# Rescheduled side steps in a fused attention and token-mixing kernel: an added stop and an early drain in the last groups, a later third weighing part in the first, two more warm-up matmuls

## The chip, the cores and the metric

The kernel runs on one core of a Trainium2 chip. The metric is the device time of one execution in microseconds (us), the median of several runs. Engines are called TensorE (PE; its weight loads are PEld), VectorE (DVE), ScalarE (ACT), GpSimd (POOL) and SyncE (SP, which here only issues DMAs).

## What is computed

x is 2048 tokens by 1024, in bf16. It is normalised row by row, and three things are added:

```
xn  = layernorm(x)
out = x + A(xn) + B(xn)

B: h = layernorm(xn)                        # [2048, 1024]
   u = gelu(h.T @ w1 + b1)                  # [1024, 3584]
   y = u @ w2 + b2                          # [1024, 2048], transposed back

A: q, k, v = xn @ wq, xn @ wk, xn @ wv      # 32 heads of 32, 4 segments of 512 tokens
   per segment s:  p = softmax(q k.T * scale + causal mask)
                   a_dot = p v
                   a_mem = phi(q) M / (phi(q) z + 1e-6)
                   o_s = g * a_mem + (1 - g) * a_dot,  g = sigmoid(beta)
                   M += phi(k).T v;  z += sum(phi(k))
   phi(t) = t + 1 for t > 0, exp(t) else
   A = concat(o_s) @ wo
```

## The kernel before, in words

**Stages.** One core does all of it in one program. First come warm-up matmuls on a tile of zeros (N_WARM of them, 512 columns each, lines 529 to 531), while x and the first columns of w1 arrive. The layer norm makes h chunk by chunk, and the first hidden columns are multiplied as chunks come (early_hidden: 16 chunks, 8 matmuls for each in eight PSUM banks). Then the token-mixing products follow (two large matrix products in a seven-product scheme) up to about 351 us. The rest is attention, the function that the change edits.

**Attention.** A unit u is one segment (u // 8) and one group of four heads (u % 8), 32 units in all. TensorE's work for a unit is of two kinds:

- The unit's own attention: logits(u, step) writes four banks (0 to 3) with q k.T, ScalarE takes the exponential of them into pT (line 1216), and GpSimd clears what the causal mask forbids (line 1220). weigh(u, part), for part 0, 1 and 2, multiplies pT with the values, and from segment 1 on also pqT (phi of q) with the memory MZbf. Parts 0 and 2 use bank 4, part 1 uses bank 5. Each part ends with a VectorE copy from the bank to ost (line 1267); part 2 also updates the memory M in the first three segments. weigh(u - 1, ...) runs in unit u, one unit late.
- Dense jobs of eight 512-column matmuls each, kept in a queue (jobs): q_job and k_job (projections for unit u + 2), v_job, and wo_job(c, half), half of the output projection of token chunk c. Jobs take banks 6 and 7 in turn. Each job ends with a copy out of its bank: ScalarE for q and most v, VectorE for k (kT, line 1112), for the v of m = 1 and 2 (vA, line 1142), and for the output job (fin, line 1158, a sum with the rest of the result; its second half then issues the output DMA and loads the fin of two chunks later).

**Side steps.** The small VectorE work that follows weigh is a queue of closures, side. For unit u - 1 in segments 1 to 3 combine gives four: scales (three small operations, lines 1308 to 1310), products(0) and products(1) (prod, line 1314), and add (o_s, line 1320), which also issues the DMA that transposes o_s into oT. In segment 0 there are two. Between the first and the rest stands phi_q(u) (lines 1080 and 1082, the result is pqT, which weigh(u, 0) reads one unit later). At the end come phi_k(u + 1) with the DMA transpose into pk, and in some units the scaling of a chunk of x for the next segment (xs, line 986) with its DMA transpose (xn). From u = 23 on the phi_k step is still queued but does nothing.

**What sets the order.** The order is written out by the program as it is built; each engine then runs its own list in that order. dense(n) issues n matmuls of the queue of jobs. Where side is not empty and dense was not called with side=False, it stops within a job at the places that the job's stops name, after 1, 4 and 7 matmuls (STOPS) or after 1 and 4 (STOPS_DVE), and takes one step from side at each. A unit's matmuls are cut into pieces by the shares given to cut, and logits and weigh stand between the pieces: cuts[0], logits 0, cuts[1], weigh 0, cuts[2], weigh 1, cuts[3], weigh 2, then the new steps are queued, cuts[4], logits 1, and so on. Only cuts[0] and what follows weigh 2 may take steps. Steps that find no stop are left over for the next unit.

**Output jobs.** Those of segment 2 (chunks 8 to 11) run in units 27 to 31: chunk 8 in 27 and 28, 9 in 29 and 30, 10 in 30 and 31, 11 in 31. After unit 31 what is left in side is issued, and tail() does the last unit's weighing, combine and transposition, and the output products of segment 3. Its first two products, into banks 6 and 7, need the oT of groups 24 to 29; the next ones that of 30, and the last that of 31.

A wait is set per tile and per bank: an operation waits for the last writer of what it reads and for the readers of what it overwrites.

Of the kernel before, what the change touches and what calls it, by code (L numbers as in the profile page):

```python
# [30 lines left out]
N_UNIT = N_SEG * N_GRP  # L31
# [353 lines left out]
class _Kernel:  # L385
    SB_BASE = 16512
    SB_END = 229344
    LEAD = 2
    N_WARM = 10
    G_AT = 3584  # L390
    B_AT = G_AT + 7 * 14336

# [104 lines left out]
    def consts(self):  # L497
# [31 lines left out]
        with fw.group(reads=[self.R_warm], writes=[self.R_bank[0]]):  # L529
            for _ in range(self.N_WARM):  # L530
                fw.mm(self.bank(0), self.warm[:, 0:P], self.warm[:], start=True, stop=True)
# [617 lines left out]
    def wo_job(self, c, half):  # L1149
        s = c // 4  # L1150

        def mm(b, j):
            self.fw.mm(self.bank(b), self.oT[s % 2][:, j, (c % 4) * P:(c % 4 + 1) * P],
                       self.wo[:, j, half * 512:(half + 1) * 512], start=(j == 0), stop=(j == N_GRP - 1))

        def end(b):
            dst, R = self.fin[c % 4][:, half * 512:(half + 1) * 512], self.R_fin[c % 4][half]
            self.fw.op("dve", lambda e: e.tensor_tensor(dst, self.bank(b), dst.bitcast(F16), op=ALU.add),  # L1158
                       reads=[self.R_bank[b], R], writes=[R])
            if half == 1:  # L1160
                self.fw.dma(self.out_d[:, c, :], self.fin[c % 4][:], reads=self.R_fin[c % 4], is_output=True)
                self.load_fin(c + 2)

        return [0, None, lambda: [self.R_wo] + self.R_oT[s % 2], mm, end, self.STOPS_DVE]

    def load_fin(self, c):
        if c < N_TCH:
# [186 lines left out]
    def attention(self):  # L1354
        self.jobs, self.turn = deque(), 0
        self.side = deque()
        self.exps, self.in_etmp = [], [None] * 4
        self.wo_plan = {}
        for s in range(N_SEG - 1):
            at = [N_GRP * s + 10 + n for n in range(8)] if s < 2 else [27, 28, 29, 30, 30, 31, 31, 31]  # L1360
            for n, u in enumerate(at):
                self.wo_plan.setdefault(u, []).append((4 * s + n // 2, n % 2))
        self.jobs.extend([self.q_job(0), self.k_job(0)] + [self.v_job(0, c) for c in range(4)])
        self.dense(16)
        self.late_exps()
        self.phi_k(0)
        self.k_transpose(0)
        self.jobs.extend([self.q_job(1), self.k_job(1)])
        self.dense(100)
        self.load_fin(0)  # L1370
        self.load_fin(1)
        for u in range(N_UNIT):
            even = u % 2 == 0
            self.jobs.extend(self.unit_jobs(u))
            total = 8 * len(self.jobs) - sum(j[0] for j in self.jobs)
            c = 4 * (u // N_GRP + 1) + u % N_GRP
            xn = u % N_GRP < 4 and c < N_TCH
            if xn:
                self.xn_load(c)
            cuts = self.cut(total, (0, 4, 2, 2, 2, 14, 8) if even else (7, 3, 2, 2, 2, 16))  # L1380
            self.dense(cuts[0])
            self.logits(u, 0)
            self.dense(cuts[1], False)
            if u:
                self.weigh(u - 1, 0)
            self.dense(cuts[2], False)
            if u:
                self.weigh(u - 1, 1)
            self.dense(cuts[3], False)
            if u:  # L1390
                self.weigh(u - 1, 2)
                steps = self.combine(u - 1)
                last = steps[-1]
                steps[-1] = lambda u=u, last=last: (last(), self.o_transpose_dma(u - 1))
                self.side.append(steps.pop(0))
            if N_GRP <= u:
                self.side.append(lambda u=u: self.phi_q(u))
            if u:
                self.side.extend(steps)
            if u + 1 < N_UNIT:  # L1400
                self.side.append(lambda u=u: (self.phi_k(u + 1), self.k_transpose(u + 1)))
            if xn:
                self.side.append(lambda c=c: (self.xn_scale(c), self.xn_transpose(c)))
            self.dense(cuts[4])
            self.logits(u, 1)
            if even:
                self.dense(cuts[5])
                self.logits(u, 2)
            self.dense(100)
        while self.side:  # L1410
            self.side.popleft()()
        self.tail()
# [82 lines left out]
```

## Time and profile before

| what | value |
|---|---|
| runs | 663.57, 663.70, 662.08 us; median 663.57 |
| the profiled execution's own time | 663.34 us |
| its span (first to last instruction) | 661.6 us |
| mean granted TensorE clock | 0.997 |
| TensorE busy | 646.4 us (98%) |
| VectorE busy | 426.3 us (64%) |
| ScalarE, GpSimd busy | 276.0 us (42%), 144.9 us (22%) |
| attention starts, ends | about 351 us, 661.6 us |

The span is that of one profiled execution; the time of an execution is a little longer (1.74 us here). A row of a group or of the order of time names line, engine, operation and the tiles written and read; ps_all is PSUM. All matmuls carry line 198, that of a helper, so they are told apart by their tiles: "ps_all<-wo,oT" is an output job, "ps_all<-vA,pT" a weighing, "ps_all<-qT,kT" logits, "ps_all<-warm" the warm-up. Matmuls overlap: one of 512 columns is shown with 379 ns, but the next starts 0.216 us after it. Some matmul records are missing from the trace, so that a count can be one or two short. "[0.39 <-DVE kT L1112]" after a row means that the engine was idle for 0.39 us before it, until that instruction released it.

### The profile page before, as it was taken

The numbers are of one execution on the slowest core, as the hardware profiler recorded it, in microseconds if no ns is written. First come the engines' busy times: TensorE is split into PE (matmuls) and PEld (weight loads), VectorE is DVE, ScalarE is ACT, GpSimd is POOL, SyncE is SP. The second block draws the span as 40 slices with busy tenths as digits, with TensorE's granted clock in tenths as the row PEclk, the third lists the DMA queues.
The fourth block names the chain that finished last, engine by engine and source line by source line (L and its number), as shares of the span: only waits on it lengthen the run. The fifth ranks groups of instructions, "written<-read, shape, count | busy, mean of one in ns | idle before, by whom it ended". The sixth has DMA issues, their size and how long they took to land.

```text
span 661.6 us, 11057 instructions
## 1 busy us (share of the span) xinstructions
PE 646.4 (98%) x4567; PEld 303.1 (46%) x4622; DVE 426.3 (64%) x821; ACT 276.0 (42%) x297; POOL 144.9 (22%) x181
## 2 busy tenths in 40 slices
PE   8999999999999999999999999999999999999978
PEld 3444444444444444444444444444444444544434
DVE  6965675665643554244522576689888998777875
ACT  7442232332300000000012777886676776667730
POOL 2500000000020222112220333333333333233320
PEclk9999999999999999999999999999999999999989
DMA  9704242242647645755285687558545685444133
GB/s 318 192 0 128 64 118 73 65 127 64 165 137 206 159 122 133 192 167 135 66 223 183 164 176 115 127 132 174 128 113 118 160 157 127 120 104 85 47 119 96
DMA packets 187242, 87.65 MB, mean 132 GB/s; under 512 B 116024, under 2 KB 174392, under 8 KB 187192
## 3 DMA queue, kind: packets, MB, share of 16 engines
q1 hardware_dynamic: 187048, 86.91, 52.2%
q8 instruction: 36, 0.59, 0.4%
q14 instruction: 14, 0.11, 0.0%
q10 hardware_dynamic: 144, 0.03, 0.0%
HBM read 67.13 MB, written 8.39 MB: 114 GB/s over the span
## 4 chain that ended last, share of the span: by engine, by line
PE 94%; DVE 2%; DMA 2%; issue 1%; ACT 1%; SPq 0%; DVEq 0%
PE ps_all L198 94%; DMA xs<-in_A_x_dram 1%; DMA w1early<-in_B_w_dram 1%; ACT pT L1216 1%; DVE fin L1442 1%; DMA oT<-o_s 0%; DVE vA L1142 0%; DVE ost L1267 0%; SPq L220 0%; DVE fin L1158 0%; DVE xs L986 0%; DVE o_s L1320 0%; DVE pqT L1082 0%; DVE mtmp L1080 0%; DVE prod L1314 0%
## 5 line engine op out<-in xcount | busy, mean ns | idle before, releaser
L1216 ACT ACTIVATE pT<-ps_all 128x2048 bf16<-128x2048 f32 x80 | 150.1, 1876 | 57.4 <-PE ps_all L198 57.3
L1220 POOL TENSOR_SCALAR_AFFINE_SELECT pT<-pT 128x512 bf16<-128x512 bf16 x128 | 96.4, 770 | 197.4 <-ACT pT L1216 197.4
L690 DVE TENSOR_TENSOR part<-ps_all,part 128x512 f32<-128x512 f32 x76 | 52.5, 691 | 119.0 <-PE ps_all L198 118.2
L926 POOL TENSOR_TENSOR part<-part,stg 128x512 f32<-128x512 f32 x24 | 33.0, 1402 | 266.2 <-DVE part L690 266.2
L695 ACT ACTIVATE part<-ps_all 128x512 f32<-128x512 f32 x20 | 11.9, 597 | 149.0 <-PE ps_all L198 149.0
L742 ACT ACTIVATE g<-part,b1c 128x512 f16<-128x512 f32 x36 | 26.0, 722 | 98.9 <-DVE part L690 98.9
L198 PE MATMUL ps_all<-wo,oT 128*128 128x512 bf16 (+2 forms) x254 | 62.8, 374 | 4.1 <-DMA oT<-o_s 3.1
L198 PE MATMUL ps_all<-wv,xnT 128*128 128x512 bf16 x238 | 65.2, 379 | 1.6 <-issue 0.6
L198 PE MATMUL ps_all<-xnT,wq 128*128 128x512 bf16 x248 | 62.0, 380 | 0.8 <-DVE kT L1112 0.4
L1267 DVE CAST ost<-ps_all 128x396 bf16<-128x396 f32 (+2 forms) x96 | 44.6, 476 | 26.8 <-PE ps_all L198 25.1
L198 PE MATMUL ps_all<-xnT,wk 128*128 128x512 bf16 x245 | 59.6, 379 | 1.5 <-issue 1.4
L198 PEld LDWEIGHTS ps_all<-vA,pT 128*128 128x128 bf16 x1280 | 45.0, 96 | 21.4 <-DVE ost L1267 4.4
L198 PE MATMUL ps_all<-g,sum 128*128 128x512 f16 x224 | 51.0, 379 | 0.0
L198 PE MATMUL ps_all<-g,w2s 128*128 128x512 f16 x224 | 51.0, 379 | 0.0
L198 PE MATMUL ps_all<-vA,pT 128*128 128x33 bf16 x1280 | 48.6, 178 | 1.4 <-DVE pqT L1082 1.0
L198 PE MATMUL ps_all<-gT,sum 128*128 128x512 f16 x224 | 49.7, 379 | 0.0
L198 PE MATMUL ps_all<-h,sum 128*128 128x512 f16 x192 | 45.2, 379 | 0.0
L198 PE MATMUL ps_all<-h,w1s 128*128 128x512 f16 x192 | 44.9, 379 | 0.0
L198 PE MATMUL ps_all<-hT,sum 128*128 128x512 f16 x192 | 43.6, 379 | 0.0
L1314 DVE TENSOR_TENSOR prod<-ost,srec 128x512 bf16<-128x512 bf16 x48 | 39.6, 826 | 0.8
L198 PEld LDWEIGHTS ps_all<-xnT,wk 128*128 128x128 bf16 x256 | 23.8, 98 | 29.8 <-issue 3.2
L198 PEld LDWEIGHTS ps_all<-wo,oT 128*128 128x128 bf16 x272 | 23.8, 99 | 29.1 <-issue 11.2
(99 smaller groups left out, 806.0 us busy)
## 6 DMA issues: line engine op xcount, KB each, us to landing
w2s<-in_B_w_dram SPq DMA_DIRECT2D x8, 1792.0 KB, 8.5
w1s<-in_B_w_dram SPq DMA_DIRECT2D x12, 1024.0 KB, 5.6
wq<-in_A_wq_dram SPq DMA_DIRECT2D x32, 256.0 KB, 3.3
wk<-in_A_wk_dram SPq DMA_DIRECT2D x32, 256.0 KB, 3.3
stg<-in_A_x_dram SPq DMA_DIRECT2D x16, 256.0 KB, 2.9
xs<-in_A_x_dram SPq DMA_DIRECT2D x16, 256.0 KB, 3.4
out_dram<-stg SPq DMA_DIRECT2D x16, 256.0 KB, 3.0
fin<-out_dram SPq DMA_DIRECT2D x16, 256.0 KB, 3.6
```

The costliest lines, as they stand in the source:

```text
L198: ins = self.nc.tensor.matmul(*args, **kwargs)
L690: self.fw.op("dve", lambda e: e.tensor_tensor(self.tmp[dst][:], self.bank(b), self.tmp[src][:], op=ALU.add), reads=[self.R_bank[b], self.R ...
L695: self.fw.op("act", lambda e: e.activation(self.tmp[dst][:], self.bank(b), ACT.Copy), reads=[self.R_bank[b]], writes=[self.R_tmp[dst]])
L742: self.fw.op("act", lambda e: e.activation(self.gB[f % 2][half][:, f // 2, :], src, ACT.Gelu_apprx_tanh, bias=self.b1c[:, f:f + 1], scale= ...
L926: fw.op("pool", lambda e: e.tensor_tensor(self.tmp[t][:], self.tmp[t][:], self.stg[k][:, 512 * half:512 * half + 512], op=ALU.add), reads= ...
L1216: fw.op("act", lambda e: e.activation(dst, src, ACT.Exp, scale=SCALE), reads=self.R_bank[0:4], writes=[R[v % 2][kb] for v, kb, _ in blocks ...
L1220: fw.op("pool", lambda e: e.affine_select(d, d, pattern=[[0, 4], [1, P]], compare_op=ALU.is_ge, fill=0.0, base=0, channel_multiplier=-1), ...
L1267: fw.op("dve", lambda e: e.tensor_copy(dst, src), reads=[self.R_bank[b]], writes=[self.R_ost[o][part]])
L1314: fw.op("dve", lambda e: e.tensor_tensor(self.prod[:, n, :], ost[:, n, 0:D_HEAD], rec[:, n].unsqueeze(2).to_broadcast([P, 16, D_HEAD]), op ...
L1442: fw.op("dve", lambda e: e.tensor_tensor(dst, self.ps[:, b, c0:c1], dst.bitcast(F16), op=ALU.add), reads=[self.R_bank[b], R], writes=[R])
```

## The change

There are four edits. N_WARM goes from 10 to 12. The output jobs of chunks 9 to 11 take STOPS, with a stop after the seventh matmul, in place of STOPS_DVE. In units 0 to 9 the shares of cut put two more matmuls between the second and the third weighing part: cuts become 0, 3, 1, 4, 0, 10, 6 (before: 0, 3, 1, 2, 2, 10, 6) in even units and 5, 3, 1, 3, 1, 11 (before: 5, 3, 1, 1, 2, 12) in odd ones, of 24 matmuls. In units 28 to 31 the piece between logits 0 and the first weighing part may take steps, and what then still stands in side is issued ahead of the first weighing part.

```diff
-    N_WARM = 10
+    N_WARM = 12
...
-        return [0, None, lambda: [self.R_wo] + self.R_oT[s % 2], mm, end, self.STOPS_DVE]
+        return [0, None, lambda: [self.R_wo] + self.R_oT[s % 2], mm, end, self.STOPS if c >= 9 else self.STOPS_DVE]
...
-            cuts = self.cut(total, (0, 4, 2, 2, 2, 14, 8) if even else (7, 3, 2, 2, 2, 16))
+            if u < 10:
+                cuts = self.cut(total, (0, 4, 2, 4, 1, 13, 8) if even else (7, 3, 2, 4, 1, 15))
+            else:
+                cuts = self.cut(total, (0, 4, 2, 2, 2, 14, 8) if even else (7, 3, 2, 2, 2, 16))
+            end = u >= N_UNIT - 4
             self.dense(cuts[0])
             self.logits(u, 0)
-            self.dense(cuts[1], False)
+            self.dense(cuts[1], end)
+            while end and self.side:
+                self.side.popleft()()
             if u:
                 self.weigh(u - 1, 0)
```

## The prediction

> **What bounds the kernel now.** I read the share lines of the page first, then the chain of waits from 615 us to the end, the table by stage with the granted clock, and TensorE's order of time in the first groups and in the first 10 us.
>
> ```profile
> PE   8999999999999999999999999999999999999978
> PE 94%; DVE 2%; DMA 2%; issue 1%; ACT 1%; SPq 0%; DVEq 0%
> ```
>
> TensorE is the bound: only its waits, and its time at half clock, can be won. Those at the end:
>
> ```profile
> 630.25 0.69 DVE fin L1158
> ...
> 632.64 0.70 DVE pqT L1082
> 633.35 0.05 issue
> 633.39 1.84 PE ps_all L198 x46
> ...
> 638.33 0.73 DVE o_s L1320
> 639.06 0.03 DVE fin L1158
> 639.09 2.43 DMA oT<-o_s
> 641.52 0.25 issue
> 641.76 5.18 PE ps_all L198 x39
> ```
>
> First column start, second length. Before 633.39 weigh(30, 0) waits for pqT of group 30, whose two VectorE operations stand behind an output job's fin. Before 641.76 the tail's first product waits for oT of group 29, whose add (o_s) ended at 639.06.
>
> ```profile
> 632.20:633.40 1.20, 0.18 (x2) 0.01 (x1) 1.17 (x3) 1.20 (x1) 0.26 (x1) 1.00 0.00 0
> 638.50:641.76 3.26, 0.19 (x1) 0.03 (x1) 3.16 (x8) 0.00 (x0) 1.05 (x2) 0.99 0.30 79
> 641.76:645.13 3.37, 3.37 (x8) 1.14 (x9) 1.28 (x3) 0.00 (x0) 0.00 (x0) 0.50 0.52 157
> ```
>
> Stretch, length, busy PE, PEld, DVE, ACT, POOL, then the granted clock. After the idle 3.26 us the clock is 0.50 for 3.37 us. The same half rate stands at the start, where no clock record exists, in the spacing of the weight loads, 0.43 us until 10.13 and 0.21 after:
>
> ```profile
> 9.71 0.15 PEld L198 LDWEIGHTS ps_all<-h,w1early 128*128 128x128 bf16 x1 [0.28 <-DVE ln_st L588]
> 10.13 0.81 PEld L198 LDWEIGHTS ps_all<-h,w1early 128*128 128x128 bf16 x4 [0.28 <-issue]
> ```
>
> And in the first groups (third weighing part is the x16; the x1 before it is the projection's matmul):
>
> ```profile
> 374.00 0.38 PE L198 MATMUL ps_all<-xnT,wq 128*128 128x512 bf16 x1
> 374.47 0.57 PE L198 MATMUL ps_all<-vA,pT 128*128 128x33 bf16 x16
> ...
> 387.59 0.97 DVE L986 TENSOR_SCALAR xs<-xs,ln_mv,ln_rs 128x1024 bf16<-128x1024 bf16 x1 [1.95 <-DMA xs<-in_A_x_dram]
> 388.48 0.68 DVE L1112 CAST kT<-ps_all 128x512 bf16<-128x512 f32 x1
> ...
> 389.30 0.38 PE L198 MATMUL ps_all<-xnT,wq 128*128 128x512 bf16 x1 [0.39 <-DVE kT L1112]
> ```
>
> A 512-column matmul takes 0.216 us of TensorE (start to start), so 374.00 could have been followed at 374.22: 0.25 us of waiting for the ost copy that frees bank 4.
>
> [...] 10.25, 641.72 and 645.13 are whole multiples of 3.413 us apart (185 and 1). [...] the add at 638.33 stands behind prod at 637.61 and fin at 637.00. [...] o_s takes 0.73 us while POOL's select runs (638.33) and 0.41 without (628.26).
>
> **The change part by part.** I wrote out the order of both versions by hand from dense, cut and STOPS.
>
> *Last groups.* Groups 28 and 29 keep their order, as the job of chunk 9 in group 29 has only an empty step to hand out. From group 30: add28 runs in the stretch before weigh(29, 0); scales29, phi_q30, prod0 and prod1 of 29 all fall in group 30, add29 in the first matmul of group 31, and the five steps of 30 in group 31. Before, group 31 began with six steps left over, and group 30's own came only ahead of the tail.
> - pqT of 30: VectorE has scales29 (0.74 us) and phi_q30 (0.97) done by about 629.5, before weigh(30, 0) is reached at 632.2. The 1.18 us at 633.39 goes.
> - oT of 29: add29 at about 631.3 behind prod1 and fin of wo10.0; with issue to landing 2.4 us, landed near 634.2. The 3.24 us ahead of 641.76 goes, and with it the half clock: 12 products took 4.24 us (641.76 to 646.00) in place of 12 x 0.216 = 2.59, so 1.65.
> - New: add28 (0.42) now precedes the ost copy of weigh(29, 0), which ended just in time for weigh(29, 2) at 625.69: 0.07. fin of wo10.1 (0.61 to its successor) now stands at 632.5 ahead of the ost copy of weigh(30, 0): weigh(30, 2) waits 0.22, as at 619.69 (0.22, same pair).
> - New: the tail's second product writes bank 7, which the last output job leaves (120 jobs alternate 6 and 7). Its fin stands behind prod0, prod1 and add of 30. From ost30 2 at 634.45: scales 0.8, phi 0.95, fin of wo11.0 0.65, two prods 1.4 to 1.8, add 0.4 to 0.7, fin 0.7 ends at 639.5 to 640.2. The first product is through at 638.95, so a wait of 0.55 to 1.3; I take 0.9.
> Sum: 1.18 + 3.24 + 1.65 - 0.07 - 0.22 - 0.9 = 4.9 us, between 4.4 and 5.3. Hidden: phi_q31 and oT of 30 (landed about 642, wanted after 645). SP's queue gets oT of 29 and of 30 ahead of the output DMAs of chunks 10 and 11 that they followed; those reads are wanted after 648. What is late next is that fin.
>
> *First groups (units 0 to 9).* The part two matmuls (0.43 us) later covers the 0.25 us waits in units 1, 5 and 7 and the 0.12 in unit 3: 0.87. The steps each start a stop or two later; in units 1 and 3 the xn step is left to the next unit. So xs for chunk 6 is loaded ahead of xn5's transpose on SP (1.3 us, issued 380.45) in place of behind it, and its landing at 387.6 comes some 1.5 us earlier. That takes all or nothing of the 0.54 us wait at 389.30; I take 0.4. The pk transposes come about 0.65 us later; that of group 2 was issued at 379.13, lands within 5 us, and is used at 390.57. Units 10 to 12 carry one step more, in by unit 13: nothing, as VectorE idles 28 us between 436 and 624 (159.33 of 187.70 busy); without that, one prod, 0.83. In even units the vA cast (0.69) now comes ahead of the third ost copy; no TensorE wait is behind it until the next unit. Sum 1.3, between 0.5 and 1.4.
>
> *Warm-up.* Ten end at 5.70, TensorE idles 1.06 us and starts at 6.76 when w1early lands (6.67). Two more at 0.43 end at 6.55, so they lie in idle time and cost nothing (were it gone, 0.85). What they can bring: the window 3.43 to 6.84 was idle 31% and did not release the clock; it would be idle 6%. If that passes, the release comes at 6.84 and not at 10.25: 3.41 / 2 = 1.7 us. The data would keep up (chunk 1 of h is ready at 8.44, needed at 6.76 + 8 x 0.216 = 8.49; w1early for chunk 2 lands at 9.41, needed at 10.2). [...] Bounds 0 and 1.8; I take 1.6 as the likelier.
>
> **Sum.** The profiled execution is 663.34 us, 661.6 of span and 1.74 around it. It holds both half-rate stretches, and lies 0.2 below the median of the runs, 663.57; the run at 662.08 may have missed one. 663.34 - 4.9 - 1.3 - 1.6 = 655.5; I add 0.4 for small waits of the size of those found at 619.69 that I did not see: 655.9.
>
> **The rivals.**
> - *No earlier release.* All the rest holds, the clock still comes at about 10.2 us: 655.9 + 1.6 = 657.5. For it: whether 6% idle passes is not in the trace. Chance 0.32.
> - *The wait moves to bank 7.* VectorE's chain of group 30 slips by 2 to 3 us [...], TensorE idles near 3.4 us between the first two products, and half clock comes with it: 655.9 + 2.5 + 1.6 = 660. Against it: VectorE has idle time at 629 to 630 in the trace. Chance 0.10.
> - *The change does not do what it says.* The third stop finds no step, "none left over" fails (add29 is left over still), and only the first groups gain: 662. Chance 0.03.
> - *Slower.* The later phi_k steps send the pk transposes so late that weigh part 2 waits in each of the ten first units. Decides once pk comes over 6 us later than now; at 1.3 us in each unit 13 us come on top of 655.9, 669. Against it: the delay is 0.65 us. Chance 0.03.
>
> **How the numbers follow.** The forecast, 655.9, has a chance of 0.52, its own range 654.7 to 656.9. To 8 in 10 the range takes in the first rival and part of the second: 654.6 to 659.0. A measurement of this kernel tells 0.3% (2 us) from no change. Faster by more: forecast, first, second rival, 0.94; within: the third, 0.03; slower: 0.03.
>
> **What would show it.** Right: no PE wait at weigh(30, 0); a short wait between the first two products of the tail with fin L1158 as releaser; no 0.50 clock near 640 us; no wait before the x16 of units 1 to 7; loads at 0.21 us spacing from about 7 us. Wrong: a PE gap over 2 us after 635 us, or new waits in units 1 to 12.

## The result and the profile after

| | median, us | runs |
|---|---|---|
| before, run beside it | 663.14 | 4, 662.08 to 663.70 |
| changed | 658.17 | 4, 657.67 to 659.62 |

The ratio is 0.993, with a 95% interval of 0.991 to 0.9951: some 5 us faster, 2.3 us less than predicted, and inside the range. The profiled execution of the changed kernel is the slowest of its four, 659.62 (span 657.9), so the two profiles differ by 3.72 us. Its page has, in the rows that the prediction showed:

```profile
PE   7999999999999999999999999999999999999988
...
PEclk8999999999999999999999999999999999999999
...
PE 92%; DVE 6%; issue 1%; DMA 1%; ACT 0%; SPq 0%; DVEq 0%
```

The end of the busy row has filled up, its first digit has fallen, and the clock row has an 8 there: this execution ran part of its start at half rate (granted clock 0.50 from 7.47 to 10.85, in the windows below). In the shares of the chain DMA lost a point and VectorE gained four. TensorE's waits from 350 us on show why (what released it; then us in total, times, longest). The kernel before:

```profile
PE ps_all L198 <- DMA oT<-o_s: 3.1, 1, 3.1
...
PE ps_all L198 <- DVE pqT L1082: 1.0, 1, 1.0
```

The changed kernel:

```profile
PE ps_all L198 <- DVE fin L1158: 1.2, 1, 1.2
PE ps_all L198 <- DVE kT L1112: 0.9, 1, 0.9
PE ps_all L198 <- ACT pT L1216: 0.5, 2, 0.4
PE ps_all L198 <- DVE ost L1267: 0.3, 1, 0.3
```

Both waits that the last groups' edits bear on are gone. The row for pT stands in both profiles. Of the new ones, that for fin and that for ost were predicted, that for kT in unit 13 was not. The changed kernel's chain near the end, in the part that answers to 630 to 642 us of the chain before:

```profile
632.48 0.79 DVE o_s L1320
633.27 0.60 DVE fin L1158
633.88 0.49 DVE ost L1267
634.36 0.05 issue
634.41 0.65 PE ps_all L198 x17
...
637.22 0.68 DVE fin L1158
637.90 0.61 DVE prod L1314
638.53 1.01 DVE prod L1314
639.54 0.02 issue
639.57 0.74 DVE o_s L1320
640.30 0.61 DVE fin L1158
640.92 0.05 issue
640.96 7.46 PE ps_all L198 x72
```

There is no DMA in it any more. Twice TensorE now waits for a VectorE queue that works without a break: for the ost copy behind add and fin (ends 634.36), and for the fin that frees bank 7 behind two prods and an add (ends 640.92). In TensorE's order of time:

```profile
634.41 0.57 PE L198 MATMUL ps_all<-vA,pT 128*128 128x33 bf16 x16 [0.29 <-DVE ost L1267]
...
635.74 4.06 PE L198 MATMUL ps_all<-wo,oT 128*128 128x512 bf16 x18
640.96 1.47 PE L198 MATMUL ps_all<-wo,oT 128*128 128x512 bf16 x6 [1.17 <-DVE fin L1158]
```

The first scores matmul of each unit is a good mark for an account by stage. Columns: when it starts in the two profiles, and the difference, all in us.

| mark | before | after | difference |
|---|---|---|---|
| unit 0 | 364.41 | 365.04 | +0.63 |
| unit 8 | 424.92 | 424.09 | -0.83 |
| unit 11 | 451.36 | 450.53 | -0.83 |
| unit 12 | 459.17 | 458.69 | -0.48 |
| unit 14 | 478.15 | 478.64 | +0.49 |
| unit 31 | 631.23 | 631.76 | +0.53 |
| first transposition in the tail | 651.99 | 648.27 | -3.72 |

So in these two executions the start lost 0.63, the first groups won 1.46, **units 11 to 13 gave 1.32 of it back**, and the end won 4.25. The start is no loss of the schedule: the twelve warm-up matmuls were through earlier than ten had been, and the data came later. Windows of the changed kernel (columns as in the prediction; the last two, the share of the DMA engines and GB/s, are not used here):

```profile
1.25:5.37 4.12, 4.12 (x12) 1.43 (x12) 1.74 (x4) 2.24 (x5) 0.29 (x1) 1.00 0.78 235
5.37:7.47 2.10, 0.00 (x0) 0.03 (x1) 1.16 (x4) 1.19 (x2) 0.55 (x1) 0.99 0.99 331
7.47:10.85 3.38, 3.38 (x9) 1.15 (x10) 3.30 (x11) 3.12 (x5) 1.31 (x3) 0.50 1.03 366
```

The clock record of this execution begins at 4.02 with full rate, in the middle of the warm-up; ahead of the record the clock column shows 1.00, although the warm-up's weight loads lie 0.43 us apart there (1.65 to 3.79), as they do at the clock of 0.50 (7.85 to 10.41). The rest of the warm-up ran at double speed (four loads from 4.12 take 0.75 us, some 0.2 apart) and ended at 5.37, TensorE idled 2.10 us, and the clock fell back to half for the first 3.38 us of work.

### The profile page after: what moved, and what is told of

Same layout as the page of the kernel before. It is cut to its first block, busy times and chain, and to the rows that moved or that the text cites. A ratio compares the mean times of both kernels' runs of the same rounds, so it can differ in the third digit from the quotient of the medians.

```text
span 657.9 us, 11118 instructions
## 1 busy us (share of the span) xinstructions
PE 648.8 (99%) x4624; PEld 303.1 (46%) x4624; DVE 426.7 (65%) x821; ACT 275.9 (42%) x297; POOL 146.6 (22%) x181
## 4 chain that ended last, share of the span: by engine, by line
PE 92%; DVE 6%; issue 1%; DMA 1%; ACT 0%; SPq 0%; DVEq 0%
PE ps_all L198 92%; DVE prod L1314 1%; DVE fin L1158 1%; DMA xin<-in_A_x_dram 1%; DVE fin L1448 1%; DVE ost L1267 0%; DVE mtmp L1082 0%; DVE mtmp L1080 0%; DVE o_s L1320 0%; DVE pqT L1082 0%; ACT pT L1216 0%; DVE srec L1309 0%; DVE xs L986 0%; DVE kT L1112 0%; DVE srec L1308 0%
## 5 line engine op out<-in xcount | busy, mean ns | idle before, releaser
L1220 POOL TENSOR_SCALAR_AFFINE_SELECT pT<-pT 128x512 bf16<-128x512 bf16 x128 | 98.1, 783 | 195.5 <-ACT pT L1216 195.5
L198 PE MATMUL ps_all<-wv,xnT 128*128 128x512 bf16 x256 | 68.5, 380 | 0.9 <-DVE kT L1112 0.9
L198 PE MATMUL ps_all<-wo,oT 128*128 128x512 bf16 (+2 forms) x272 | 65.8, 367 | 1.2 <-DVE fin L1158 1.2
L198 PE MATMUL ps_all<-xnT,wq 128*128 128x512 bf16 x256 | 63.6, 380 | 0.0
L198 PE MATMUL ps_all<-xnT,wk 128*128 128x512 bf16 x256 | 61.8, 380 | 0.0
```

Source lines behind the costliest of these rows:

```text
L198: ins = self.nc.tensor.matmul(*args, **kwargs)
L1220: fw.op("pool", lambda e: e.affine_select(d, d, pattern=[[0, 4], [1, P]], compare_op=ALU.is_ge, fill=0.0, base=0, channel_multiplier=-1), ...
```

## The experiments

**My theory** after the result: the end is as predicted, short by two VectorE queues; the first groups gain 1.3 to 1.5, but those of units 8 and 9 leave a step over that units 11 to 13 pay for; the warm-up gains only where it shifts the clock's windows. **Rivals**: what is lost in units 11 to 13 belongs to other edits; the end's gain comes from one of its two edits alone; the half clock is not worth 1.65.

The medians of the kernel before beside these runs were 661.83, 661.93 and 663.01 on three chips (35, 18 and 11 runs), so I compare ratios, and stretches of the profiles. Where a text of what was expected speaks of groups, it means units.

**The warm-up alone** (kernel before, one edit).

```diff
-    N_WARM = 10
+    N_WARM = 12
```

> The kernel before with twelve warm-up matmuls and nothing else. My theory: they lie in TensorE's idle time ahead of the first hidden columns and cost nothing; they win up to 1.7 us only where the clock is released early and stays released until the data come, which the trace of the changed kernel denies for one phase (released at 4.02 us, half again at 7.43). So 0 to 1.0 us faster in the median, and all 32 groups as in the kernel before. Rival, the forecast's step: an idle share of 6% passes, and nearly every run is 1.6 us faster. Second rival: no phase gains, and the time is that of before within 0.3 us.

Measured: 661.34, ratio 0.998 [0.9971, 0.9989]. By the interval that is 0.7 to 1.9 us of 661.83, between the medians only 0.5. It is not an equal step in each execution. The times of the kernel before lie in clusters: 1 at 659.52, 18 from 660.98 to 661.86, 16 from 662.73 to 663.85. With twelve matmuls 7 lie from 659.52 to 660.27, 14 from 661.08 to 662.26 and 1 at 662.86. So executions with ten seem to have had the early release often: their profiles show it at 10.25 (kernel before), but at 5.83 (the first groups alone) and 5.84 (the emptying alone). The mean granted clock tells of something else. It does not take in what lies ahead of the first release: in the profile before, half rate up to 10.25 and for 3.37 us near the end would make it 0.990, the 3.37 us alone 0.997, and 0.997 is shown. So the 7 runs with a mean of 1.0 (1 of the 35 before) are runs without the half-rate stretch near the end. Why twelve matmuls make those more frequent is not shown.

**The first groups alone** (kernel before, new shares for u < 10).

```diff
-            cuts = self.cut(total, (0, 4, 2, 2, 2, 14, 8) if even else (7, 3, 2, 2, 2, 16))
+            if u < 10:
+                cuts = self.cut(total, (0, 4, 2, 4, 1, 13, 8) if even else (7, 3, 2, 4, 1, 15))
+            else:
+                cuts = self.cut(total, (0, 4, 2, 2, 2, 14, 8) if even else (7, 3, 2, 2, 2, 16))
```

> The kernel before with the new shares in groups 0 to 9 alone. My theory: 1.4 to 1.5 us are won by the logits of group 8, and 1.3 us of it are given back between the logits of groups 11 and 14, as the steps that no longer fit in groups 8 and 9 push VectorE's copies late; so 0.1 to 0.2 us in all. Rival, the forecast's step: the one step more is hidden by VectorE's idle time, and 1.3 to 1.5 us are kept to the end; the loss in groups 11 to 13 of the changed kernel came from another edit or from chance.

Measured: 661.92, ratio 1.0005 [0.9991, 1.0019], **no gain**. Against the profile before it wins 1.46 from unit 0 to unit 8, nothing to unit 11, and gives back 1.31 by unit 14.

Of the 1.46, 0.40 hangs on the execution. It is the 0.39 us wait at 389.30 in the profile before, where xs came late: VectorE began on it 23.18 us after the first scores matmul of unit 0, and 21.39 to 21.44 us after it in the five other profiles with the old shares (the warm-up, the last groups, the filled stretch, the third stop and the emptying alone). Unit 3 takes 6.88 us in the profile before and 6.47 or 6.48 in those five. Against four of them the edit wins 1.06 (1.20 against the last groups alone), some 0.27 in each of the units 1, 3, 5 and 7, and it gives back 1.31. That fits a time without gain.

The new wait is in it as in the changed kernel, so it belongs to this edit:

```profile
469.41 0.59 PE L198 MATMUL ps_all<-wv,xnT 128*128 128x512 bf16 x2 [0.85 <-DVE kT L1112]
```

**The last groups alone** (kernel before, both their edits).

```diff
-        return [0, None, lambda: [self.R_wo] + self.R_oT[s % 2], mm, end, self.STOPS_DVE]
+        return [0, None, lambda: [self.R_wo] + self.R_oT[s % 2], mm, end, self.STOPS if c >= 9 else self.STOPS_DVE]
...
+            end = u >= N_UNIT - 4
...
-            self.dense(cuts[1], False)
+            self.dense(cuts[1], end)
+            while end and self.side:
+                self.side.popleft()()
```

> The kernel before with the third stop and the drain alone. My theory: nothing moves up to the logits of group 29; from those of group 31 to the last transposition TensorE is 4.2 to 4.3 us faster than in the profile of before, of which some 1.65 are the half clock; the tail's second product waits 1.3 us for bank 7. In time 2.7 to 4.3 us faster. Rival: the gain is the avoided half clock alone, 1.6 us, since the new wait for bank 7 and the one behind fin in group 31 take the rest.

Measured: 657.67, ratio 0.9934 [0.9917, 0.9951]: nearly the whole of the change. From the first scores matmul of unit 31 to the first transposition in the tail it takes 16.50 us, 20.76 before and 16.51 in the changed kernel.

**The new shares only in units 0 to 7** (changed kernel).

```diff
-            if u < 10:
+            if u < 8:
```

> The changed kernel, with the new shares in groups 0 to 7 only; groups 8 and 9 are cut as before. My theory: the backlog that groups 8 and 9 leave is the cause of the wait of 0.8 us at 471.46 and of the 0.3 us in group 11; with it gone, the 1.3 us of groups 11 to 13 are not lost, and the time is 1.2 to 1.3 us below that of the changed kernel. Rival: groups 8 and 9 have nothing to do with it, and the time is that of the changed kernel; a part of the gain of the first groups may even be lost, 0.2 us slower.

Measured: 656.02, ratio 0.9906 [0.989, 0.9922]. Between units 0 and 8 it wins the same 1.46, and at unit 14 it has all of it. The median is 2.15 below that of the changed kernel, where 1.2 to 1.3 was expected; the two come from different sets of runs, and the profiles show 1.3 for this stretch. The place that waited in the changed kernel, in this one:

```profile
467.16 0.40 PE L198 MATMUL ps_all<-qT,kT 32*128 32x512 bf16 x4
467.49 0.39 PE L198 MATMUL ps_all<-wo,oT 128*128 128x512 bf16 x1
467.71 0.59 PE L198 MATMUL ps_all<-wv,xnT 128*128 128x512 bf16 x2
```

VectorE tells the reason. In this kernel:

```profile
465.24 0.28 DVE L1080 TENSOR_SCALAR mtmp<-etmp 128x512 bf16<-128x512 bf16 x1
465.56 0.69 DVE L1082 SCALAR_TENSOR_TENSOR mtmp<-kT,mtmp 128x512 bf16<-128x512 bf16 x1
466.17 0.68 DVE L1112 CAST kT<-ps_all 128x512 bf16<-128x512 f32 x1
```

In the changed kernel, where the phi_k step carried over (the first two rows) now stands in unit 12 ahead of that unit's own steps:

```profile
463.31 0.28 DVE L1080 TENSOR_SCALAR mtmp<-etmp 128x512 bf16<-128x512 bf16 x1
463.63 0.69 DVE L1082 SCALAR_TENSOR_TENSOR mtmp<-kT,mtmp 128x512 bf16<-128x512 bf16 x1
...
468.95 0.72 DVE L1080 TENSOR_SCALAR mtmp<-etmp 128x512 bf16<-128x512 bf16 x1
469.71 1.00 DVE L1082 SCALAR_TENSOR_TENSOR mtmp<-kT,mtmp 128x512 bf16<-128x512 bf16 x1
470.63 0.68 DVE L1112 CAST kT<-ps_all 128x512 bf16<-128x512 f32 x1
```

and GpSimd there:

```profile
468.75 1.42 POOL L1220 TENSOR_SCALAR_AFFINE_SELECT pT<-pT 128x512 bf16<-128x512 bf16 x2 [2.38 <-ACT pT L1216]
```

Relative to the scores matmul of unit 13 the kT copy begins 0.99 us ahead of it here (466.17 to 467.16) and 0.74 us behind it in the changed kernel (469.89 to 470.63). In both kernels a phi_k stands right ahead of the copy that frees the k job's bank. With one step more ahead of it, it starts 0.98 us later against that matmul (0.94 us ahead of it in place of 1.92), and it fell beside the causal select, where it took 1.68 us from start to the copy's start in place of 0.93. The copy began 2.35 us after TensorE had left the k job (the next job starts at 468.28), against 0.62 in this kernel (465.55), and the next projection, which takes that bank, waited 0.85.

**The bank of the tail's second product** (the kernel of the experiment before, one edit): bank 0, which the last scores have left, in place of bank 7, which the third product takes.

```diff
-            i, h, b = n // 2, n % 2, (6, 7, 0, 1, 2, 3, 5, 4)[n]
+            i, h, b = n // 2, n % 2, (6, 0, 7, 1, 2, 3, 5, 4)[n]
```

> The changed kernel, with the new shares in groups 0 to 7 only, and with the tail's second product in bank 0 and its third in bank 7. My theory: the wait for fin ahead of the tail's second product (1.33 us at 640.96 in the profile after) is one for bank 7 alone, so it goes; from the logits of group 31 to the last transposition 15.2 us in place of 16.5, and the time is 1.2 to 1.3 us below that with the shares alone (656.0), near 654.7. Rival: VectorE is the bound of the tail (fin, combine of group 31), the wait turns up at the third product or at the transposition, and 16.5 us stay.

Measured: 654.95, ratio 0.9893 [0.9878, 0.9909]. The wait for fin is gone; the two products run through:

```profile
632.64 0.40 PE L198 MATMUL ps_all<-qT,kT 32*128 32x384 bf16 x8
632.97 5.35 PE L198 MATMUL ps_all<-wo,oT 128*128 128x512 bf16 x24
638.16 0.26 PE L198 MATMUL ps_all<-vA,pT 128*128 128x33 bf16 x4
```

From unit 31 to the transposition it takes 15.15 us, 1.35 less than the 16.50 of the experiment before. No version that was run is faster, and its interval lies below that of the changed kernel (0.991 to 0.9951).

**Sixteen and twenty warm-up matmuls** (the kernel just told, N_WARM 12 to 16 and to 20).

> The same as the kernel with bank 0, with sixteen warm-up matmuls. My theory from the windows seen so far (released after windows that were 81% busy and more, not after 64%; half again after 35 and 37%, kept at 43%): twelve are already enough in most phases, sixteen only close the case in which the array falls back before the data come (one profile after), and they hold up the first hidden columns by up to 0.7 us where the release comes late; the median is the same within 0.4 us. Rival: [...] more warm-up still brings 0.5 us and more in the median.

> The same with twenty. My theory: the clock is released between 3.9 and 7.3 us whatever comes after, so twenty end at 6.9 to 8.6 us, past the 7.0 us at which the data are there; 0.4 to 0.9 us slower in the median than with twelve. Rival [...]: faster than twelve, or the same.

Measured: 655.42, ratio 0.9898 [0.9883, 0.9914], and 654.95, ratio 0.9897 [0.9881, 0.9912]: no difference from twelve that these runs can tell (the medians of sixteen and twelve are 0.47 apart, the ratios 0.0005). Twenty were to cost 0.4 to 0.9 and did not. In their profiles twenty are followed by the first product at 7.73, and twelve leave TensorE idle until 7.51, when the data came: a loss of 0.2. The release between 3.9 and 7.3 us that was expected was my estimate from the windows that the expectation of sixteen lists; the two profiles with twelve whose windows are shown here have it at 4.02 and 4.46. The expectation had the data there at 7.0; in the profiles whose TensorE waited for them, the first product starts between 6.76 and 7.51.

**Half clock priced by itself** (kernel before, with 13 matmuls more into a bank that is free at that time, ahead of the tail's first product; nothing reads what they write).

```diff
+        with fw.group(reads=[self.R_ident, self.R_wo], writes=[self.R_bank[5]]):
+            for _ in range(13):
+                fw.mm(self.bank(5), self.ident[:], self.wo[:, 0, 0:512], start=True, stop=True)
         product(0, 0, 6)
```

> The kernel before, with thirteen matmuls of 512 columns into the free bank 5 ahead of the tail's first product: 2.8 us of additional work, whose result nobody reads, in the idle 3.24 us. It prices the half clock by itself. My theory: the idle time is too short to be won otherwise, so the only difference is that no half-rate window follows: clock 1.0 in the records of nearly all runs, and 1.3 to 1.7 us faster in the median although more is computed. Rival: the half clock near 640 us has another cause than the idle time (or costs nothing, as the tail waits for VectorE), and the time is the same or up to 0.3 us slower.

Measured: 659.99, ratio 0.9969 [0.9958, 0.9981], so 1.3 to 2.8 us **faster with more work**.

```profile
638.55 2.97 PE L198 MATMUL ps_all<-wo,ident 128*128 128x512 bf16 x13
641.80 2.75 PE L198 MATMUL ps_all<-wo,oT 128*128 128x512 bf16 x12 [0.28 <-DMA oT<-o_s]
644.38 0.26 PE L198 MATMUL ps_all<-vA,pT 128*128 128x33 bf16 x4
```

The transposed block comes at the same time as before, and the 12 products take 2.58 us (641.80 to 644.38) at a granted clock of 1.00, in place of 4.24 at 0.50 for the first 3.37 us: 1.66, where the prediction had 1.65. Of the 13 runs 12 have a mean granted clock of 1.0, of the 18 of the kernel before beside them one. The wait and the half clock are thus separate terms, and the second is caused by the first.

**The third stop alone, and the emptying alone** (kernel before with one of the last groups' two edits each).

> The kernel before with the third stop of the last four groups alone, without the emptying of the remainder ahead of each group. Theory: the third stop is what matters. With it the pq of group 30 is ready within its own group and the output job of group 29 is through ahead of the last group's end, so its transposed block lands before the tail's second product; both long waits (for pqT 1.18 us and for oT 3.24 us) are gone with this alone, the time from the first scores matmul of group 31 to the first transposition of the tail is 16 to 17 us (20.76 before, 16.50 with both edits), and the time is that of both edits together, 657.7, or up to 0.7 us less. Rival: the emptying is needed as well; the wait for oT stays in part, that stretch is 18.5 us or more and the time 659.5 or more.

> The kernel before with the emptying of the remainder ahead of each of the last groups alone, two stops an output job as before. Theory: the emptying brings the leftover addition out ahead of the group's weighing, so this alone also removes both long waits, and the two edits do not add up: the stretch from the first scores matmul of group 31 to the first transposition of the tail is 16 to 17 us, the time 657 to 658.5, with 0.5 to 1 us of new wait of a group's third weighing part behind the emptied additions. Rival: without the third stop group 30's pq is still late; the stretch is 18.5 us or more and the time 659.5 or more.

Measured: 658.63, ratio 0.9936 [0.9923, 0.995], and 658.59, ratio 0.9946 [0.9925, 0.9967]; the stretch of the end takes 17.40 and 16.86 us. **Each edit alone removes both long waits**, and does nearly all that the two do together (16.50). What is left differs. With the third stop alone TensorE waits as follows, for the third weighing part and for the tail's second product:

```profile
634.53 0.57 PE L198 MATMUL ps_all<-vA,pT 128*128 128x33 bf16 x16 [1.00 <-DVE ost L1267]
...
641.27 1.47 PE L198 MATMUL ps_all<-wo,oT 128*128 128x512 bf16 x6 [1.16 <-DVE fin L1158]
```

With the emptying alone:

```profile
633.43 0.57 PE L198 MATMUL ps_all<-vA,pT 128*128 128x33 bf16 x16 [1.48 <-DVE ost L1267]
...
639.14 1.47 PE L198 MATMUL ps_all<-wo,oT 128*128 128x512 bf16 x6 [0.33 <-DVE fin L1158]
```

The stretch of the third stop alone is 0.4 over what the theory allowed, and its time 0.9: I had seen only the wait for fin, and its third weighing part waits 1.00 as well, its ost copy standing behind two prods of 1.98 and a fin. With the emptying alone that wait is 1.48, where 0.5 to 1 was expected, and the time is 0.1 over. (The kernel before is 1.2 slower in this set than in that of the two edits together, so the ratios are the better comparison: 0.9936 and 0.9934.) The order of the same VectorE work decides which of the two waits it becomes.

## Why the prediction was right, and where it was not

*Last groups, predicted 4.9.* Right in its mechanism; it measured 4.25. Both waits and the half clock are gone, and the half clock measured 1.66 by itself. The two waits that it added were sized too small. That for bank 7 was put at 0.55 to 1.3 with 0.9 taken (its own summands give 0.4 to 1.1), and is 1.33 between the two products (640.96 less 639.63, when the next matmul was due: 635.74 + 18 x 0.216). The third weighing part waits 0.45 (634.41 less 633.96) where 0.22 was taken. Together that is 0.66, what is missing. Behind the second stands o_s, which ran at 632.41 to 633.28 and not at about 631.8 (the 631.3 of the prediction, and this profile's unit 31 starts 0.53 later).

A likely cause for that delay: beside GpSimd's selects (629.40 to 631.34 and from 631.78) the two prods took 2.16 us as a pair and o_s 0.87; without a select beside them they took 1.41 (641.24) and 0.41 (628.26) in the profile before. The rows of mtmp above show longer times for two other operations beside the select at 468.75, 0.72 for 0.28 and 1.00 for 0.69. What makes them longer is not shown.

*First groups, predicted 1.3.* The direct part is right: 1.46 from unit 0 to unit 8, in the changed kernel and in two experiments. Of it 1.06 is won against most other profiles with the old shares too, where the prediction had 0.87. The other 0.40 is the wait for xs: the prediction priced it right for its profile (0.4), but that is the only one of six with the old shares that has it. **The step that failed** is "Units 10 to 12 carry one step more, in by unit 13: nothing, as VectorE idles 28 us". The prediction named the other case, "one prod, 0.83". It was neither. The additional step pushed a phi_k, and with it a kT copy, past the time at which TensorE needed the bank: 0.35 of smaller waits in unit 11 and 1.01 in unit 13, less 0.04 in unit 12, 1.32 in all, more than that 1.06. Idle time summed over a stretch, here 28 us, said nothing of the one place where a bank had to come free: there VectorE was busy for 6.01 of the 6.15 us from 465.75 to 471.90, and the kT copy came only behind the phi_k ahead of it (469.71 to 470.71). That the step is shown and not only argued: with the old shares in units 8 and 9 the loss is gone, and the time is 656.02.

*Warm-up, predicted 1.6.* Inside what the edit alone measured, 0.7 to 1.9, but not a step that each execution takes. In the changed kernel's profiled execution it brought nothing, as the clock fell back, and loads at 0.21 us spacing, which were to show it from about 7 us, begin at 10.84. Its other three runs have a mean granted clock of 1.0, so no half-rate stretch after the first release, and are 1.4 to 2.0 us shorter. The rival *No earlier release*, 657.5, is the nearest in time, but not for its reason: in the profile of the warm-up alone the clock was released after a window that was 94% busy (1.05 to 4.46, 3.21 of 3.41 us).

*The sum.* Before the 0.4 for unseen waits the prediction had 655.5. With 0.65 less at the end, and 0.14 (1.46 less 1.32) in place of 1.3 in the first groups, it is 657.3; the median is 658.17. What is left, 0.9, may lie in the warm-up, which alone measured 0.7 to 1.9 and had 1.6 in the sum; the runs do not settle it. The median misses the forecast's own range, 654.7 to 656.9, and lies in the wider one, which was drawn to take in the rival just named. It came to lie there for other reasons, the loss in units 11 to 13 and the two waits at the end, and that is luck.

## What to carry to other kernels

When side work is moved by a slot, follow the surplus to the place where it is absorbed: what counts is which bank or buffer the delayed copy frees, not the engine's idle total (here 28 us, beside a loss of 1.32). Removing the long wait near the end here (3.24 us) also removed the half clock that followed it (1.66), and both belong in the sum. A wait that one profile shows need not be the kernel's: look for it in a second one before it is counted as a gain. After the removal of a wait look at which VectorE operation frees the next bank: here another bank for the next product took 1.35 us from that stretch.

## What the runs showed of the hardware

*The clock.* In the records of the two main profiles the clock is 1.00 or 0.50, and its changes, the first release among them, lie 3.41 us or a whole multiple of it apart: at 4.02, 7.43 and 10.85 in the changed kernel, at 10.25, 641.72 and 645.13 in the kernel before. Stretches of this length are called windows here. The clock changed after windows that were neither wholly busy nor wholly idle. Each window below begins or ends at a change of the clock in the record. Two windows of the changed kernel (columns as above):

```profile
0.61:4.02 3.41, 2.77 (x7) 1.04 (x8) 0.81 (x4) 1.49 (x2) 0.54 (x3) 1.00 0.62 189
4.02:7.43 3.41, 1.35 (x6) 0.39 (x4) 2.37 (x7) 2.39 (x4) 0.55 (x1) 1.00 0.91 296
```

After the first, 81% busy (2.77 of 3.41 us), the clock was released; after the second, 40% busy (1.35), it fell back. In the kernel with only the warm-up changed:

```profile
639.34:642.76 3.42, 2.52 (x7) 0.88 (x8) 2.18 (x4) 0.00 (x0) 0.00 (x0) 0.50 0.51 157
...
4.46:7.88 3.42, 1.65 (x8) 0.58 (x7) 3.17 (x10) 2.05 (x4) 1.10 (x2) 1.00 0.99 299
```

After the first, 74% busy, the clock was not released (it stayed at 0.50 to 646.17); after the second, 48% busy, it was not lost (the mean granted clock, 0.995, is what the 6.83 us from 639.34 to 646.17 make alone). In the kernel with only the last groups changed, it was lost after a window 42% busy (mean granted clock 0.997):

```profile
4.32:7.74 3.42, 1.42 (x8) 0.46 (x7) 2.87 (x8) 2.28 (x5) 0.89 (x2) 1.00 0.99 312
```

Of the windows shown here the least busy with a release after it was 81% busy and the busiest that left the clock at half 74%; the busiest with a loss after it was 42% busy, and the least busy that kept full clock 48%. This is busy time as the profile shows it, where the last matmul ahead of a pause counts with 0.379 us; with 0.216 the shares of the windows at the start are 35, 37 and 43% for the 40, 42 and 48 given here, as in what was expected of sixteen matmuls. The windows do not begin at the same time in each execution: with ten warm-up matmuls the first release came at 4.32, 4.38, 5.83, 5.84 and 10.25 in five profiles (in the first two the clock fell back at 7.74 and 7.79; in the second it is 0.50 from there to 11.20), so that ten sometimes did as well as twelve.

*More work was faster.* Thirteen matmuls that nobody reads, in an idle stretch of 3.24 us, won 1.3 to 2.8 us.
